# Lent softmax tiles, later weight passes on ScalarE, and low parts on VectorE in an attention and two-layer kernel

## The chip, the cores and the metric

The kernel runs on one core of one Trainium2 chip. The metric is the device time of one execution in microseconds (us). The core has TensorE (matrix products), VectorE and ScalarE (elementwise work and reductions), GpSimd (elementwise work, on-chip memory only) and SyncE, whose queue issues every transfer of this kernel. Each engine runs its own instructions in order, and engines wait for each other by semaphores. In the rows they are PE (PEld is its loading of weights), DVE, ACT, POOL and SP.

## The reference

Attention over `q`, `k`, `v` of shape (4, 8, 576, 64), as the sum of two branches, and then two feed-forward layers over the 2304 tokens, 512 wide with 2048 hidden columns:

```python
# pooled branch: means of 4 neighbours, dense softmax attention over 144 positions, repeated 4 times
out_up = np.repeat(sm_attn(q_d, k_d, v_d), 4, axis=2)
# local branch: softmax over the positions closer than 4
mask = np.abs(pos[:, None] - pos[None, :]) < 4
out_local = softmax(where(mask, scale * q @ k.T, -1e9)) @ v
x = (out_up + out_local)            # (4 * 576 tokens, 512)
h = x @ moe_w_in;  r = np.maximum(h, 0.0);  x = (r * r) @ moe_w_out
h = x @ moe2_w_in; g = h * np.cos(h);       y = g @ moe2_w_out
```

The feed-forward weights arrive as 64-bit floats. The kernel makes of each a 32-bit value and splits it in a high and a low part, and splits the inputs of each product likewise: three products (high by high, high by low, low by high) stand for one.

## The kernel before, in words

**Tokens and blocks.** The local branch works in 36 windows of 64 query tokens, the pooled branch in 16 units (4 batches by 4 head pairs, `down`). The first layer takes the tokens in five blocks of 8, 7, 7, 7 and 7 windows (512 or 448 tokens), and for each block its 16 groups of hidden columns: 80 steps. A step is `stage_a` (line 691: the hidden block, 12 products), `gelem1` on ScalarE (relu in line 715, square in 716, high copy `gh` in 703), `low` on VectorE (line 709, `gl`), and one step or two later `stage_b1` (line 774, 12 products). The second layer follows from about 540 us on.

**Block one comes first.** Before the 80 steps a loop advances all of block one's tasks together, one piece of each in a pass: `pool(0)`, `early_v` (loads of the values and the pooled values' sums, line 283), four `down` units, eight `window` tasks and the conversion of the first three weight blocks. A window is: scores on TensorE (lines 455 and 465), maximum on VectorE (line 339), exponentials on ScalarE (lines 343 or 354), sums and reciprocals on VectorE (356, 477, 478), normalisation on GpSimd (479), transposes (489), a copy (492), the product with the values (510), and on VectorE the sum with the pooled branch (`xt`, line 526); every second window then gives the high part `xh` (537) and the low part `xl` (538) of the layer's input. The product with the values waits until all four `down` units of the batch are done. A window holds a tile `pr` (four there are) from its exponentials to its transposes and a tile `pt` (two) from there to the product of line 510. The sums of line 283 are queued behind the latest traced maximum:

```python
        with behind("max"):
            nc.vector.tensor_reduce(out=vp[...], in_=places[hp]..., op=ALU.add, axis=AX.X)
```

`behind(*names)` puts an instruction behind the last traced one of the first of these names that exists, on the same engine; no semaphore is added by it.

**Weights.** `conv1(f)` loads one raw block of the first layer (1 MB, line 550, two buffers) and `split` converts it: line 564 on ScalarE (a first pass over the upper words), lines 566, 569 and 571 on VectorE (clamp, shift, join with the lower words), line 577 on ScalarE (the high part), line 584 on GpSimd (two subtractions of 128x512, the low parts). The raw buffer is free after line 571. Low parts go to rings of three and five buffers (`LO_RING`) and are also written to memory (line 609), from where the later blocks load them. Blocks 0 to 2 belong to the loop before the steps, blocks 3 to 15 are started at steps 0 to 11. `conv2` does the same with the second layer's weights in steps 18 on, with its low part in line 580 on GpSimd.

**Order.** The program is traced in the order of the Python loops; the framework's planner then orders each engine's queue by a simulated timeline, keeping the order that `behind` asks for. `gelem1` is traced with high priority. The flag `early[0]` is true until the loop for block one has ended. The tiles `gt`, `gl` (two each) and `gh` (three) are the first layer's g tiles, 128x512; the first of them is asked for by step 0.

Of the kernel before, what the change touches and what calls it, by code (L numbers as in the profile page):

```python
# [8 lines left out]
F32 = mybir.dt.float32  # L9
F32R = mybir.dt.float32r  # L10
BF16 = mybir.dt.bfloat16
U32 = mybir.dt.uint32
AF = mybir.ActivationFunctionType
ALU = mybir.AluOpType
# [4 lines left out]
P = 128  # L19
# [4 lines left out]
HPAIR = H // 2  # L24
WQ = 64
WK = WQ + 2 * HALO
# [8 lines left out]
TMAX = 512  # L35
# [31 lines left out]
def window_of(w):  # L67
    b, i = divmod(w, NWB)
    t0 = i * WQ
    k0, k1 = max(t0 - HALO, 0), min(t0 + WQ + HALO, S)  # L70
    return b, i, t0, k0, k1
# [3 lines left out]
def kernel(  # L75
# [11 lines left out]
    nc = tc.nc  # L87
# [4 lines left out]
    gp = ctx.enter_context(tc.tile_pool(name="gp", bufs=3))  # L92
# [9 lines left out]
    cm = cm_pool.__enter__()  # L102
# [10 lines left out]
    for t, v in zip(magic, (MAGIC, -MAGIC)):  # L113
# [9 lines left out]
    caps = {  # L123
        "a": 3, "h": 1, "acc": 4, "qkw": 3, "vw": 3, "pr": 4, "pt": 2, "xt": 2, "qp": 1, "xd": 2, "vp": 1, "av": 3, "pl": 2, "raw": 2,
        "dpr": 2, "dpt": 1, "qk0": 0,
    }
    used = dict.fromkeys(caps, 0)
    now = [-1]
    early = [True]
    kinds = {}  # L130
    last = {}

    def need(name, n=1):
        while early[0] and name in SPREAD:
            if name not in ("qk0", "pl") and used[name] < caps[name]:
                used[name] += 1
                held.setdefault(name, []).append(None)
                return
            if spare:
                held.setdefault(name, []).append(spare.pop(0))  # L140
                return
            other = LENT.get(name)
            if other and used[other] < caps[other]:
                used[other] += 1
                held.setdefault(name, []).append(other)
                return
            yield
        while used[name] + n > caps[name]:
            yield
        used[name] += n  # L150

    def done(name, n=1):
        f = taken[name].pop(0) if early[0] and name in SPREAD else None
        if f is None:
            used[name] -= n
        elif f in caps:
            used[f] -= n
        else:
            spare.append(f)
# [15 lines left out]
    def need_a(n=1):  # L175
        while True:
            free = ["a"] * (caps["a"] - used["a"])
            if early[0]:
                free += [t for tag in ("h", "acc") for t in [tag] * (caps[tag] - used[tag])]
            if len(free) >= n:  # L180
                break
            yield
        got = []
        for tag in free[-n:]:
            used[tag] += 1
            t = {"a": ps_a, "h": ps_h, "acc": ps_acc}[tag].tile([P, 512], F32, tag=tag, name="ps_" + tag)
            kinds[id(t)] = (tag, t)
            got.append(t)
        return got

    def done_a(*ts):
        for t in ts:
            used[kinds.pop(id(t))[0]] -= 1
# [230 lines left out]
    def x_tiles(j):  # L424
        while j > 1 and now[0] < NF * (j - 1) - 1:
            yield
        if j not in xblk:
            xblk[j] = tuple(xp.tile([P, NK, TMAX], F32R, tag=t, name=t) for t in ("xh", "xl"))
        return xblk[j]

    def window(w):
        b, i, t0, k0, k1 = window_of(w)
        n, off = k1 - k0, HALO - (t0 - k0)
# [11 lines left out]
            yield  # L445
        if not early[0]:
            yield
        yield from need("pr")
        while apart and len(whole) < 2 * HPAIR:
            yield  # L450
        s, = yield from need_a()
# [18 lines left out]
                    done("qk0")  # L470
        else:
            done("qkw")
        mx = cm.tile([P, 2, HPAIR], F32, tag="mx", name="mx", bufs=4)
        pr = cm.tile([P, HPAIR, WK], F32, tag="pr", name="pr", bufs=caps["pr"])
        prv = pr[:, :, :n]
        yield from exps(s, sv, mx, prv, SCALE, w % 2 == 0 if apart else w < W0[2])
        nc.vector.tensor_scalar_add(out=mx[:, 1], in0=mx[:, 1], scalar1=1e-9)
# [2 lines left out]
            out=prv, in0=prv, in1=mx[:, 1].unsqueeze(2).broadcast_to([P, HPAIR, n]), op=ALU.mult  # L480
        ).ins
        yield
        if not early[0]:
            yield
        yield from need("pt")
        tp, = yield from need_a()
        tpv = tp.rearrange("p (h m) -> p h m", h=HPAIR)
        for hp in range(HPAIR):
            last["pe"] = nc.tensor.transpose(tpv[:n, hp], pr[:, hp, :n], ident).ins  # L489
        done("pr")  # L490
        pt = cm.tile([WK, HPAIR, P], F32, tag="pt", name="pt", bufs=caps["pt"])
        nc.scalar.copy(out=pt[:n], in_=tpv[:n])
        done_a(tp)
        yield
# [9 lines left out]
        xh, xl = yield from x_tiles(j)  # L504
        av, = yield from need_a()
        avv = av[:, :HPAIR * WQ].rearrange("p (h m) -> p h m", h=HPAIR)
        for hp in range(HPAIR):
            for a in range(2):
# [2 lines left out]
                    avv[rows, hp], vw[:n, hp * P + a * D:hp * P + (a + 1) * D], pt[:n, hp, a * WQ:(a + 1) * WQ],  # L511
                    start=True, stop=True,
                ).ins
        done("pt")
        if not apart:
            done("vw")
        placed[0] += 1
# [2 lines left out]
        if (j, m // 2) not in xts:  # L520
# [6 lines left out]
            out=xt[:, :, (m % 2) * WQ:(m % 2 + 1) * WQ].rearrange("p h (j r) -> p h j r", r=FACTOR),  # L527
            in0=avv.rearrange("p h (j r) -> p h j r", r=FACTOR), in1=xa, op=ALU.add,
# [4 lines left out]
        if m % 2 or m == WINS1[j] - 1:  # L533
            m0 = m - m % 2
            cs = slice(m0 * WQ, (m + 1) * WQ)
            xv = xt[:, :, :(m % 2 + 1) * WQ]
            last["xh"] = nc.scalar.activation(out=xh[:, :, cs], in_=xv, func=AF.Copy).ins
            last["xl"] = nc.vector.tensor_tensor(  # L538
                out=xl[:, :, cs], in0=xv, in1=xh[:, :, cs].bitcast(F32), op=ALU.subtract
# [13 lines left out]
    def behind(*names):  # L553
        for name in names:
            if name in last:
                return tc.issue_after(last[name])
        return nullcontext()

    def split(raw, hi, los=None, sums=None):
        low, top = raw[:, :, 0], raw[:, :, 1]  # L560
        x = rawp.tile([P, 2 * DM], U32, tag="bits", name="bits")
        xv = x.bitcast(F32)
        with behind("relu", "xh", "exp"):
            nc.scalar.activation(out=xv, in_=top.bitcast(F32), func=AF.Prelu, scale=TOP_SCALE, alpha=TOP_ALPHA)
        with behind("gl", "xl"):
            nc.vector.tensor_scalar(  # L566
                out=xv, in0=xv, scalar1=TOP_MAX, scalar2=-TOP_MAX * TOP_ALPHA, op0=ALU.min, op1=ALU.max
            )
        nc.vector.tensor_scalar(out=x, in0=x, scalar1=3, scalar2=None, op0=ALU.logical_shift_left)  # L569
        yield  # L570
        nc.vector.scalar_tensor_tensor(  # L571
            out=x, in0=low, scalar=29, in1=x, op0=ALU.logical_shift_right, op1=ALU.bitwise_or
        )
        if sums:
            yield from sums(xv)
        yield "read"
        nc.scalar.activation(out=hi, in_=xv, func=AF.Copy)
        yield
        if los is None:
            nc.gpsimd.tensor_tensor(out=xv, in0=xv, in1=hi.bitcast(F32), op=ALU.subtract)  # L580
        else:
            for k, lo in enumerate(los()):
                cs = slice(k * DM, (k + 1) * DM)
                nc.gpsimd.tensor_tensor(out=lo, in0=xv[:, cs], in1=hi[:, cs].bitcast(F32), op=ALU.subtract)
        return xv

    hi1 = [None] * NF
# [108 lines left out]
    def g_tile(name, dtype=F32, tag=None):  # L696
        tag = tag or name
        return gp.tile([P, TMAX], dtype, tag=tag, name=name, bufs=3 if tag == "gh" else 2)

    def high(gt):  # L700
        n = gt.shape[1]
        gh = g_tile("gh", F32R)[:, :n]
        nc.scalar.activation(out=gh, in_=gt, func=AF.Copy)  # L703
        return gt, gh

    def low(gt, gh):
# [354 lines left out]
    for i in range(n2 + 4):  # L1061
        j, p = divmod(i, NP2)
# [104 lines left out]
```

## Time and profile before

| | |
|---|---|
| three runs | 942.91, 943.47, 943.68 us, median 943.47 |
| profiled execution | 942.37 us, its span 940.6 us |
| granted TensorE clock, mean | 0.988 |
| busy, share of span | TensorE 97%, VectorE 67%, ScalarE 62%, GpSimd 15% |
| chain that ended last | TensorE 80%, VectorE 10%, transfers 5%, ScalarE 3% |
| moved | 222.78 MB, mean 237 GB/s |

The span is from the first to the last instruction; the execution's time has some 1.8 us around it. A share of the span is an average: the start, where the attention and the conversion of weights run beside TensorE's first products, has other limits than the layers behind it. The chain is followed back from the last instruction to what released each step. A matmul's length as listed overlaps the next one's; the distance of their starts is what one takes.

### The profile page before, as it was taken

How to read it: one execution, taken by the hardware profiler on the slowest of the kernel's cores; microseconds unless marked ns; L12 is line 12 of the kernel's file. 1: busy time of each engine (PE TensorE's matmuls, PEld its weight loads, DVE VectorE, ACT ScalarE, POOL GpSimd, SP SyncE). 2: the span in 40 equal slices, each digit the busy share in tenths (PEclk: the TensorE clock that was granted, in tenths of full speed). 3: DMA queues.
4: the chain of work that ended last, by engine and by line, in shares of the span. 5: the costliest groups of instructions: out<-in, count | busy, mean ns of one | idle time of the engine just before them, and what ended most of it. 6: DMA issues, size and time to landing. Idle time of an engine off the chain costs nothing.

```text
span 940.6 us, 17687 instructions
## 1 busy us (share of the span) xinstructions
PE 913.5 (97%) x6892; PEld 834.8 (89%) x6892; DVE 634.8 (67%) x1181; ACT 579.0 (62%) x1024; POOL 144.7 (15%) x115
## 2 busy tenths in 40 slices
PE   7889979999999999999999999999999999999997
PEld 4667767888989889889899999999999999999997
DVE  7877975764567644454331158879787887888786
ACT  5677756455555555554553377777767777677674
POOL 2336642031131322222220000000000000000000
PEclk9989989999999999999999999999999999999999
DMA  9778885684889857877888886565565565665673
GB/s 232 228 239 310 293 267 175 220 304 155 311 284 316 293 183 266 306 251 260 290 299 295 270 324 208 185 197 201 184 204 190 190 211 189 206 200 186 212 237 102
DMA packets 74224, 222.78 MB, mean 237 GB/s; under 512 B 8932, under 2 KB 14436, under 8 KB 69916
## 3 DMA queue, kind: packets, MB, share of 16 engines
q1 hardware_dynamic: 74140, 221.64, 70.7%
q8 instruction: 54, 0.88, 0.4%
q14 instruction: 30, 0.25, 0.1%
HBM read 180.72 MB, written 40.89 MB: 236 GB/s over the span
## 4 chain that ended last, share of the span: by engine, by line
PE 80%; DVE 10%; DMA 5%; ACT 3%; issue 1%; SPq 0%; POOL 0%; DVEq 0%; ACTq 0%; POOLq 0%
PE ps_h L726 22%; PE acc L798 18%; PE ps_h L691 17%; PE acc L774 16%; DMA pl<-in_pool_v_dram 2%; DVE bits L571 2%; PE ps_a L510 1%; DVE bits L566 1%; DVE gl L709 1%; PE ps_a L489 1%; PE ps_a L465 1%; DMA raw<-in_w_dram 1%; DMA pl<-in_pool_qk_dram 1%; DMA qk<-in_pool_qk_dram 1%; DVE bits L569 1%
## 5 line engine op out<-in xcount | busy, mean ns | idle before, releaser
L726 PE MATMUL ps_h<-x,w2hi 128*128 128x256 f32 x1152 | 159.9, 281 | 0.0
L709 DVE TENSOR_TENSOR gl<-gt,gh 128x448 fp32r<-128x448 f32 (+1 forms) x80 | 61.2, 766 | 129.4 <-ACT gh L703 72.3
L726 PEld LDWEIGHTS ps_h<-x,w2hi 128*128 128x128 f32 x1152 | 146.6, 188 | 0.1
L798 PE MATMUL acc<-bl,gh 128*128 128x256 f32 x504 | 140.5, 280 | 0.0
L691 PE MATMUL ps_h<-xh,w1hi 128*128 128x448 f32 (+1 forms) x320 | 123.8, 388 | 2.5 <-ACT gt L715 2.5
L691 PE MATMUL ps_h<-xl,w1hi 128*128 128x448 f32 (+1 forms) x320 | 122.0, 381 | 1.8 <-DVE xl L538 1.8
L774 PE MATMUL acc<-gl,w1hi 128*128 128x448 f32 (+1 forms) x320 | 120.2, 376 | 0.7 <-DVE gl L709 0.7
L715 ACT ACTIVATE gt<-ps_h 128x448 f32<-128x448 f32 (+1 forms) x80 | 44.2, 553 | 103.3 <-PE ps_h L691 103.0
L774 PE MATMUL acc<-gh,w1hi 128*128 128x448 f32 (+1 forms) x320 | 105.9, 377 | 0.0
L798 PEld LDWEIGHTS acc<-bl,gh 128*128 128x128 f32 x504 | 95.0, 188 | 0.0
L774 PE MATMUL acc<-gh,lo 128*128 128x448 f32 x256 | 93.8, 366 | 0.0
L766 DVE TENSOR_TENSOR gl<-g,gh 128x896 fp32r<-128x896 f32 x72 | 78.2, 1086 | 11.0 <-ACT gh L761 11.0
L798 PE MATMUL acc<-w2hi,gh 128*128 128x256 f32 x288 | 80.9, 281 | 0.0
L734 ACT ACTIVATE u<-ps_h,quarter 128x512 f32<-128x512 f32 x72 | 49.4, 686 | 51.0 <-PE ps_h L726 50.7
L798 PE MATMUL acc<-w2hi,gl 128*128 128x256 f32 x288 | 80.3, 281 | 0.0
L741 DVE SCALAR_TENSOR_TENSOR r<-u,ps_h 128x512 f32<-128x512 f32 x72 | 49.4, 687 | 40.0 <-ACT u L736 34.5
L761 ACT ACTIVATE gh<-g 128x896 fp32r<-128x896 f32 x72 | 68.1, 946 | 10.7 <-DVE g L759 10.6
L746 ACT ACTIVATE r<-r,half_pi 128x512 f32<-128x512 f32 x72 | 51.8, 720 | 33.8 <-DVE r L742 33.8
L691 PEld LDWEIGHTS ps_h<-xh,w1hi 128*128 128x128 f32 x320 | 61.2, 191 | 10.8 <-ACT gt L715 3.2
L691 PEld LDWEIGHTS ps_h<-xl,w1hi 128*128 128x128 f32 x320 | 61.4, 192 | 9.2 <-DVE xl L538 2.3
L726 PE MATMUL ps_h<-x,w2lo 128*128 128x256 f32 x432 | 68.8, 281 | 0.0
L774 PEld LDWEIGHTS acc<-gl,w1hi 128*128 128x128 f32 x320 | 60.3, 188 | 7.8 <-DVE gl L709 1.1
(143 smaller groups left out, 1987.4 us busy)
## 6 DMA issues: line engine op xcount, KB each, us to landing
bl<-wo_d SPq DMA_DIRECT2D x70, 896.0 KB
raw<-in_w_dram SPq DMA_DIRECT2D x32, 1024.0 KB
lo<-lo_d SPq DMA_DIRECT2D x128, 256.0 KB
qkw<-in_win_qk_dram SPq DMA_DIRECT2D x28, 268.0 KB
pl<-in_pool_qk_dram SPq DMA_DIRECT2D x24, 288.0 KB
wo_d<-raw SPq DMA_DIRECT2D x16, 384.0 KB
out_dram<-o SPq DMA_DIRECT2D x18, 256.0 KB
lo_d<-loa SPq DMA_DIRECT2D x16, 256.0 KB
```

The lines of the kernel that those rows point to most:

```text
L571: nc.vector.scalar_tensor_tensor(out=x, in0=low, scalar=29, in1=x, op0=ALU.logical_shift_right, op1=ALU.bitwise_or)
L691: nc.tensor.matmul(h[:, :n], a[:, c * P:(c + 1) * P], x[:, c, :n], start=i == 0, stop=i == len(order) - 1)
L709: last["gl"] = nc.vector.tensor_tensor(out=gl, in0=gt, in1=gh.bitcast(F32), op=ALU.subtract).ins
L715: last["relu"] = nc.scalar.activation(out=gt, in_=h, func=AF.Relu).ins
L726: nc.tensor.matmul(h[:, s * TB:(s + 1) * TB], a[:, c * P:(c + 1) * P], x[:, c], start=i == 0, stop=i == len(order) - 1,)
L734: nc.scalar.activation(out=u, in_=h, func=AF.Identity, bias=quarter, scale=float(1.0 / (2 * math.pi)))
L741: nc.vector.scalar_tensor_tensor(out=r, in0=u, scalar=-PI2_HI, in1=hv, op0=ALU.mult, op1=ALU.add)
L746: nc.scalar.activation(out=r, in_=r, func=AF.Sin, bias=half_pi, scale=1.0)
L761: nc.scalar.activation(out=gh, in_=g[:, 1:], func=AF.Copy)
L766: nc.vector.tensor_tensor(out=gl, in0=g[:, 1:], in1=gh.bitcast(F32), op=ALU.subtract)
L774: nc.tensor.matmul(acc[d][:, :n], a, x, start=f == 0 and i == 0, stop=f == NF - 1 and i == 2)
L798: nc.tensor.matmul(o, a[:, x], b, start=opens and i == 0, stop=p == NP2 - 1 and i == 2 and (k % 2 == 1 or k == NPROD - 1),)
```

## The change

Three edits. (1) While block one is made, a window's `pr` tile may also be one of `gt`, `gt`, `gl`, `gl`, and its `pt` tile one of three `gh`; `band_tile` gives out the tiles in the order in which they come back, and the small tile `mx` of maxima and sums has eight buffers in place of four. (2) In `split`, used for both layers' weights, ScalarE's first pass is queued behind the latest high copy of g (`last["hi"]`) in place of the latest relu, and the high copy of the weights, which had no such order, behind the same. Where no g exists yet, `xh` and `exp` take its place for the first pass, as before, and `xh` for the copy. (3) The two subtractions of line 584 go to VectorE once block one's loop has ended, for weight blocks 3 to 15; blocks 0 to 2 stay on GpSimd, and so does line 580.

```diff
+    lent = {"pr": ["pr"] * caps["pr"] + ['gt', 'gt', 'gl', 'gl'], "pt": ["pt"] * caps["pt"] + ['gh', 'gh', 'gh']}
+
+    def band_tile(name, shape):
+        while early[0] and not lent[name]:
+            yield
+        if not early[0]:
+            yield from need(name)
+        tag = lent[name].pop(0) if early[0] else name
+        if tag == name:
+            return tag, cm.tile(shape, F32, tag=name, name=name, bufs=caps[name])
+        t = gp.tile([P, TMAX], F32R if tag in ("gh", "gl") else F32, tag=tag, name=name, bufs=3 if tag == "gh" else 2)
+        n = shape[1] * shape[2]
+        return tag, t.bitcast(F32)[:shape[0], :n].rearrange("p (a b) -> p a b", a=shape[1])
+
+    def band_done(name, tag):
+        if early[0]:
+            lent[name].append(tag)
+        else:
+            done(name)
...
-        yield from need("pr")
+        pr_tag, pr = yield from band_tile("pr", [P, HPAIR, WK])
...
-        mx = cm.tile([P, 2, HPAIR], F32, tag="mx", name="mx", bufs=4)
-        pr = cm.tile([P, HPAIR, WK], F32, tag="pr", name="pr", bufs=caps["pr"])
+        mx = cm.tile([P, 2, HPAIR], F32, tag="mx", name="mx", bufs=8)
...
-        yield from need("pt")
+        pt_tag, pt = yield from band_tile("pt", [WK, HPAIR, P])
...
-        done("pr")
-        pt = cm.tile([WK, HPAIR, P], F32, tag="pt", name="pt", bufs=caps["pt"])
+        band_done("pr", pr_tag)
...
-        done("pt")
+        band_done("pt", pt_tag)
...
-        with behind("relu", "xh", "exp"):
+        with behind("hi", "xh", "exp"):
             nc.scalar.activation(out=xv, in_=top.bitcast(F32), func=AF.Prelu, scale=TOP_SCALE, alpha=TOP_ALPHA)
...
-        nc.scalar.activation(out=hi, in_=xv, func=AF.Copy)
+        with behind("hi", "xh"):
+            nc.scalar.activation(out=hi, in_=xv, func=AF.Copy)
...
-                nc.gpsimd.tensor_tensor(out=lo, in0=xv[:, cs], in1=hi[:, cs].bitcast(F32), op=ALU.subtract)
+                eng = nc.gpsimd if early[0] else nc.vector
+                eng.tensor_tensor(out=lo, in0=xv[:, cs], in1=hi[:, cs].bitcast(F32), op=ALU.subtract)
...
-        nc.scalar.activation(out=gh, in_=gt, func=AF.Copy)
+        last["hi"] = nc.scalar.activation(out=gh, in_=gt, func=AF.Copy).ins
```

## Rows read from the trace of the kernel before

**Rows 1.** Stretches: PE, PEld, DVE, ACT, POOL busy us (instructions), clock, DMA share, GB/s.

```profile
12.00:50.60 38.60, 29.51 (x430) 22.63 (x428) 34.44 (x79) 26.84 (x90) 15.94 (x17) 0.91 0.83 233
...
62.00:72.00 10.00, 10.00 (x56) 7.36 (x56) 10.00 (x16) 6.46 (x18) 2.55 (x2) 1.00 0.68 212
...
90.00:100.00 10.00, 10.00 (x57) 7.57 (x55) 10.00 (x15) 7.88 (x17) 3.88 (x3) 1.00 0.67 245
...
51.00:143.00 92.00, 83.73 (x511) 65.24 (x511) 71.12 (x109) 63.74 (x155) 44.50 (x33) 0.93 0.80 271
143.00:930.00 787.00, 785.60 (x5878) 737.50 (x5877) 517.94 (x971) 483.37 (x770) 82.46 (x61) 1.00 0.70 235
```

**Rows 2.** Timeline of PE, 14 to 52 us: start, us, instruction [idle before].

```profile
23.86 1.07 PE L489 MATMUL ps_acc<-const_sb,pr 128*70 128x128 f32 x4 [0.31 <-POOL pr L479]
...
33.22 1.07 PE L489 MATMUL ps_acc<-const_sb,pr 128*70 128x128 f32 x8
...
50.62 0.80 PE L691 MATMUL ps_h<-xl,w1hi 128*128 128x512 f32 x1 [1.82 <-DVE xl L538]
```

**Rows 3.** Timeline of DVE, 19 to 31 us.

```profile
19.41 0.41 DVE L339 TENSOR_REDUCE mx<-ps_acc 128x4 f32<-128x280 f32 x1
...
26.35 0.45 DVE L339 TENSOR_REDUCE mx<-ps_acc 128x4 f32<-128x280 f32 x1 [3.46 <-PE ps_acc L465]
...
27.43 3.46 DVE L283 TENSOR_REDUCE vp<-pv 72x256 f32<-72x1024 f32 x3
```

**Rows 4.** Timeline of ACT, 126 to 134 us.

```profile
126.53 0.60 ACT L715 ACTIVATE gt<-ps_h 128x512 f32<-128x512 f32 x1
130.91 1.14 ACT L564 ACTIVATE bits<-raw 128x1024 f32<-128x1024 f32 x1 [3.78 <-DMA raw<-in_w_dram]
131.96 0.61 ACT L716 ACTIVATE gt<-gt 128x512 f32<-128x512 f32 x1
132.47 1.04 ACT L577 ACTIVATE w1hi<-bits 128x1024 fp32r<-128x1024 f32 x1
133.42 0.61 ACT L703 ACTIVATE gh<-gt 128x512 fp32r<-128x512 f32 x1
```

**Rows 5.** Timeline of DVE, 133 to 138 us.

```profile
134.07 1.39 DVE L709 TENSOR_TENSOR gl<-gt,gh 128x512 fp32r<-128x512 f32 x1 [4.50 <-ACT gh L703]
135.38 1.75 DVE L566 TENSOR_SCALAR bits<-bits 128x1024 f32<-128x1024 f32 x1
...
```

**Rows 6.** Timeline of PE, 130 to 147 us.

```profile
137.52 0.44 PE L455 MATMUL ps_a<-const_b 64*64 64x280 bf16 x2 [5.48 <-DVE xt L526]
```

**Rows 7.** Timeline of ACT, 78 to 88 us.

```profile
81.10 1.06 ACT L577 ACTIVATE w1hi<-bits 128x1024 fp32r<-128x1024 f32 x1
```

**Rows 8.** Timeline of PE, 80 to 92 us.

```profile
80.78 0.69 PE L691 MATMUL ps_h<-xh,w1hi 128*128 128x512 f32 x1 [1.82 <-ACT gt L715]
...
86.69 0.39 PE L691 MATMUL ps_h<-xh,w1hi 128*128 128x512 f32 x1
```

**Rows 9.** Groups by form, DVE, 51 to 143 us: busy us, mean ns, idle before.

```profile
L571 DVE SCALAR_TENSOR_TENSOR bits<-raw,bits 128x1024 uint32<-128x1024 uint32 x12 | 17.5, 1467 | 0.2
L566 DVE TENSOR_SCALAR bits<-bits 128x1024 f32<-128x1024 f32 x12 | 13.4, 1123 | 7.5 <-ACT bits L564 7.5
L709 DVE TENSOR_TENSOR gl<-gt,gh 128x512 fp32r<-128x512 f32 x11 | 10.8, 983 | 4.6 <-ACT gh L703 4.5
```

**Rows 10.** Groups by form, DVE, 146 to 300 us.

```profile
L571 DVE SCALAR_TENSOR_TENSOR bits<-raw,bits 128x1024 uint32<-128x1024 uint32 x7 | 8.5, 1220 | 0.1
...
L566 DVE TENSOR_SCALAR bits<-bits 128x1024 f32<-128x1024 f32 x7 | 4.8, 685 | 0.0
...
L709 DVE TENSOR_TENSOR gl<-gt,gh 128x512 fp32r<-128x512 f32 x5 | 3.4, 688 | 2.8 <-ACT gh L703 2.8
```

**Rows 11.** Groups by form, POOL, 51 to 157 us.

```profile
L584 POOL TENSOR_TENSOR loa<-bits,w1hi 128x512 fp32r<-128x512 f32 x14 | 20.0, 1429 | 44.5 <-ACT w1hi L577 19.8 <-issue 13.9 <-PE ps_h L691 5.8
```

**Rows 12.** Waits, POOL, 51 to 157 us: us in total, times, longest.

```profile
POOL loa L584 <- DMA lo_d<-lob: 4.2, 1, 4.2
```

## The prediction

> **What bounds the kernel now.** I read the table of stretches first, because a share over the whole span mixes a start that waits with a long middle that does not. From 143 to 930 us TensorE is busy 785.6 of 787.0 us at full clock [rows 1]: 1.4 us are to be had there, and nothing that the change touches there (ScalarE's passes over the second layer's weights) is late for TensorE. So the change is worth what it does before 143 us. There, from 51 to 143 us, TensorE is busy 83.73 of 92.00 us at a mean clock of 0.93 [rows 1], and before that it can't do the first layer at all, since its input is not there: the first multiplication that needs the last piece of block one's input starts at 50.62 us, after 1.82 us of waiting for VectorE [rows 2].
>
> Next the timelines of the start, for what block one's eight windows wait for. VectorE takes the maximum of window three at 19.41 us and of the next window only at 26.35 us, after 3.46 us without work, and three of the four pooled values' sums follow at 27.43 us, behind that maximum [rows 3]. The reason is in TensorE's timeline: a fifth window gets a probability tile only when one of the four in hand has been transposed, and the second of those transposes starts at 23.86 us; the third and fourth start at 33.22 us [rows 2], when a transposed tile (there are two) has been used by its product with the values. So the windows go through in pairs, and the pooled branch, which every window needs, goes through behind the third pair's maximum.
>
> The third view is the three engines around the largest wait. TensorE stands 5.48 us until 137.52 us for VectorE's sum in line 526 [rows 6]. In ScalarE's order the relu of a g block at 126.53 us is followed by the first weight pass (line 564), which waits 3.78 us for its transfer and starts at 130.91 us; the square, another block's high copy (line 577) and the copy of g follow it, the last at 133.42 us [rows 4]. VectorE waits 4.50 us for that copy, then does line 709 and line 566, and comes to line 526 after that [rows 5]. By count the pass at 130.91 us is the one for weight block 14, whereas TensorE is at block 11: it could have waited.
>
> **Part one: the lent tiles.** Four more probability tiles and three more transposed ones let all eight windows be scored, reduced and normalised before the pooled branch is done, and the pooled sums stand behind a maximum that comes sooner. The work is the same, only its order changes, so the gain is VectorE's missing work. From 12.00 to 50.60 us VectorE is busy 34.44 of 38.60 us [rows 1]: 4.2 us are free. If the order fills them and the three early weight blocks stay ahead of the input's end, the input is complete at 46.4 instead of 50.6 us. If the third block's passes (1.22 us, 0.69 us and one more like the second, as in [rows 10]: 2.6 us) fall behind it, 6.8 us are gained. Against: the maxima of windows four to seven now stand ahead of the pooled sums; at 0.45 us each [rows 3] that is 1.8 us on the pooled branch, the bound on the side of a loss. ScalarE, at 26.84 of 38.60 us [rows 1], has room for the exponentials. I take -4.2 us, since the row for it is the idle itself, and keep -6.8 and +1.8. What is late next is VectorE with no idle at all. The g tiles themselves are asked for by the first layer only after the input is complete, when all eight windows are through: no wait there.
>
> **Part two: ScalarE's passes behind the high copy.** At 126 us the order becomes relu (0.60), square (0.61), copy (0.61) [rows 4], which ends at about 128.4 us, and only then the pass that waits until 130.91 us. VectorE does line 709 before 130.3 us, 0.69 us long [rows 10]; line 566 still stands ahead of line 526, but starts when the pass ends (130.91 + 1.14 = 132.05 us) and takes 0.69 us, and line 526 can end at about 133.2 us. In the trace of before VectorE reached it at 135.38 + 1.75 = 137.13 us, and TensorE went on at 137.52. That is 4.2 us. Bounds: nothing, if another late transfer stands ahead of another relu, and 5.5 us, the whole wait [rows 6]. The price is that every first pass and high copy comes a square and a copy later, 1.2 us. Weight block 5's high copy ends at 82.16 us and its first use is at 86.69 us [rows 7, 8]: 4.5 us of cover hide it at nothing; where the cover is gone it is 1.2 us once, since the passes then follow one another at the same distance.
>
> **Part three: the low parts on VectorE.** Blocks 3 to 15 give 26 subtractions of 128x512. The same operation on the same kinds of operands takes 0.688 us on VectorE where GpSimd does nearly none of them [rows 10], so 17.9 us are added to VectorE, nearly all from 51 to 143 us. What comes back: in that stretch line 571 takes 1.467 us (1.220 later), line 566 1.123 us (0.685 later) and line 709 0.983 us (0.688 later) [rows 9, 10]. Times 12, 12 and 11 that is 3.0 + 5.3 + 3.2 = 11.5 us, and I take all of it as time in which GpSimd's subtractions held VectorE up. The net is +6.4 us on VectorE, which has 92.00 - 71.12 = 20.9 us free in the stretch; it is without a gap in 62 to 72 and in 90 to 100 us [rows 1], 20 of 92 us. I charge that share: 6.4 x 0.22 = +1.4 us. From below: -1.8 us, if the earlier low parts end the wait of 1.82 us at 80.78 us [rows 8]. From above: GpSimd stood 5.8 us for TensorE and 4.2 us for a write to memory before it could overwrite a ring buffer [rows 11, 12]; it lost nothing by that, but VectorE, waiting in the same place, would hold back line 709's low parts of g and the sums for the windows behind it, and TensorE waits for both: +10.0 us. SyncE's writes of the low parts, and the weight transfers queued behind these, come when the subtraction ends, 1.4 us after the high copy instead of 2.9 (twice 1.43, [rows 11]); I count nothing for that, since the next transfer also waits for line 571.
>
> The GPSIMD Engine Reference of the Trainium skill (section Key points) says that GpSimd shares its interfaces to the on-chip memory with VectorE, and that they contend where VectorE has two such inputs or runs in a mode with two ports. The trace agrees: line 709, with two inputs, takes 0.983 us beside GpSimd and 0.688 us without. Were the long durations due to something else that stays, VectorE would get 17.9 us instead of 6.4, the charge would be 3.9 us and the sum -4.5.
>
> **The sum.** -4.2 - 4.2 + 1.4 = -7.0 us. The profiled execution took 942.37 us with a span of 940.6; the median of the three runs is 943.47, 1.1 us more. So 942.37 - 7.0 + 1.1 = 936.5 us.
>
> **The rivals.**
> - *All of it comes.* The third block's passes fall behind the input and both waits go: -6.8 - 5.5 - 1.8 = -14.1 us, 929.4 us. For it: TensorE is short of work in no other place. Against: each place has to come out well in an order that the planner draws up anew.
> - *The weights hold.* The input is early, but the raw weights come through two buffers and one queue of transfers, and TensorE, with 4.5 us of cover at block 5, only waits for them sooner; the late transfer of 130 us stops it elsewhere. Both gains are given back and the 1.4 us stay: 944.9 us. For it: the wait at 130 us began with a transfer. Against: the weights from block 3 on are started by the first g block, so they move up with the input.
> - *VectorE waits for the ring (the other side).* A subtraction on VectorE stands before a buffer that TensorE or a write still holds, and what is behind it in the queue is what TensorE needs: +10.0 us. It falls where blocks 11 to 14 are made, so that part two's gain is not had: -4.2 + 10.0 = +5.8 us, 949.3 us. It decides once such a wait is longer than TensorE's cover, 4.5 us at block 5. For it: GpSimd's two waits of 5.8 and 4.2 us. Against: the planner knows these waits and can put other work ahead.
> - *The lending does nothing.* Windows are scored early, but the pooled branch or ScalarE sets the input's end: 0 - 4.2 + 1.4 = -2.8 us, 940.7 us.
>
> **How the numbers follow.** Forecast 0.48 (its own range 932 to 940.5 us), all of it 0.12, weights 0.17, ring 0.14, no lending 0.09. A difference under 0.2%, 1.9 us, can't be told from none: faster is below 941.6 us, slower above 945.4. Faster: 0.46 + 0.12 + 0.02 from the weights case + 0.06 from the last = 0.66. Same: 0.01 + 0.13 + 0.01 + 0.03 = 0.18. Slower: 0.01 + 0.02 + 0.13 = 0.16. The range 929 to 946 leaves out half of the first rival and most of the third, 0.06 + 0.12.
>
> **What would show it.** Part one: window seven's maximum before 24 us, no wait of VectorE near 23 us, and the first multiplication with the low part of the input near 46 us. Part two: no line 564 between a relu and its copy, and no wait of some 5 us of TensorE for line 526. Part three: line 571 near 1.22 us throughout from 55 us on, and VectorE's idle time in front of line 584 under 2 us in all; waits there of 4 us and more, with TensorE waiting for line 709 or 526 behind them, would make the forecast wrong, and so would a first multiplication no earlier than 49 us.

## The result, and the profile after

The changed kernel takes 933.72 us (median of 4 runs, 931.59 to 938.64) beside 943.58 for the kernel before on the same chip (4 runs, 942.91 to 948.2). The ratio is 0.987 [0.983, 0.991], and the difference of the medians is 9.9 us. The forecast was 936.5 with an own range of 932 to 940.5, so it came out 2.8 us faster than forecast, inside that range. Once more on another chip, run `e5_after_again` below, the ratio was 0.988 [0.985, 0.992].

The profiled execution of after is its slowest, 938.64 us with a span of 936.6. The table of stretches shows where it differs: TensorE's granted clock from 12 to 50.6 us was 0.82, beside 0.96 in `e5_after_again`, and its second hidden block starts 2.1 us later (56.30 against 54.20 us). So the profile of `e5_after_again`, the same kernel with 934.0 us and a span of 931.9, stands beside it. Numbers of the lines have moved: 691 is 711, 774 is 794, 709 is 729, 703 is 723, 715 is 735, 716 is 736, 564 is 582, 566 is 584, 571 is 589, 577 is 596, 584 is 604, 526 is 544, 537 and 538 are 555 and 556, 339 is 359, 283 is 303, 390 and 406 are 410 and 426, 455 is 475, 465 is 485, 479 is 498, 489 is 508, 492 is 510, 510 is 528.

Stretches of after (columns as in [rows 1]), the counterpart of [rows 1], with two more, from 62 to 143 and from 143 to 200 us:

```profile
12.00:50.60 38.60, 32.86 (x436) 27.73 (x435) 30.78 (x78) 26.93 (x91) 13.35 (x15) 0.82 0.79 216
...
51.00:143.00 92.00, 87.42 (x539) 68.33 (x538) 78.43 (x135) 68.78 (x154) 13.58 (x12) 0.96 0.82 285
...
62.00:143.00 81.00, 81.00 (x522) 63.65 (x522) 70.22 (x121) 62.46 (x133) 7.21 (x6) 1.00 0.82 286
...
143.00:200.00 57.00, 54.12 (x405) 45.53 (x404) 35.40 (x77) 28.41 (x70) 9.51 (x10) 1.00 0.78 263
```

The stretch of `e5_after_again` from 12 us to the end of its last `xl`, as [rows 1] ends with that of before:

```profile
12.00:46.74 34.74, 26.93 (x430) 22.41 (x427) 29.59 (x76) 25.36 (x90) 12.92 (x14) 0.95 0.82 223
```

From 62 to 143 us TensorE has no gap left (81.00 of 81.00 us at full clock). There the view of waits for before has two, the 5.48 us of [rows 6] and the 1.8 us of [rows 8]; for after it has none. These two waits cost before more than their length. Stretches of before, the whole from 62 to 143 us and one behind each wait:

```profile
62.00:143.00 81.00, 73.58 (x442) 57.35 (x442) 66.28 (x96) 54.35 (x127) 41.30 (x29) 0.94 0.81 273
81.00:84.00 3.00, 3.00 (x8) 2.32 (x8) 3.00 (x6) 2.36 (x5) 2.45 (x3) 0.50 0.85 330
138.00:141.00 3.00, 3.00 (x21) 2.48 (x18) 3.00 (x9) 1.50 (x5) 0.00 (x0) 0.50 0.90 279
```

Behind each wait the granted clock was 0.50, the lower of its two levels (1.2 and 2.4 GHz), and products of 128x512 started 0.43 us apart, where they start 0.23 us apart from 87 us and from 143 us on. By the timeline this lasts from 80.78 to about 84.3 us and from 137.5 to about 142.0; half of that, some 4 us, is an estimate of what it cost.

GpSimd's 44.50 us of work from 51 to 143 us has become 13.58, and VectorE's 71.12 has become 78.43: +7.3 by all three edits together. From 143 to 200 us TensorE is busy 54.12 of 57.00 us, where before has it busy throughout: 2.9 us are given back there, in waits of at most 1.1 us for a product's issue, GpSimd and g's copy.

Timeline of PE, `e5_after_again`, 19 to 57 us, against [rows 2]:

```profile
22.54 0.65 PE L485 MATMUL ps_acc<-qk,qk 64*64 64x70 f32 x16
...
24.10 0.92 PE L410 MATMUL ps_acc<-const_sb,dpr 96*72 96x96 f32 x6 [0.37 <-POOL pr L498]
26.30 0.41 PE L410 MATMUL ps_acc<-const_sb,dpr 96*72 96x96 f32 x3 [1.28 <-POOL pr L498]
...
29.50 3.45 PE L508 MATMUL ps_acc<-const_sb,pr 128*67 128x128 f32 x20
...
46.07 0.50 PE L711 MATMUL ps_h<-xh,w1hi 128*128 128x512 f32 x1 [1.44 <-ACT xh L555]
46.80 0.50 PE L711 MATMUL ps_h<-xl,w1hi 128*128 128x512 f32 x1 [0.23 <-DVE xl L556]
...
54.20 0.80 PE L711 MATMUL ps_h<-xh,w1hi 128*128 128x512 f32 x1 [4.57 <-ACT gt L735]
```

The windows no longer go in pairs: the last scores start at 22.54 us, the transposes of five windows run as one group of 20 from 29.50 us on, and those of the other three follow from 38.61 us. The first product with `xl` starts at 46.80 us (50.62 in [rows 2]). New is a wait of 4.57 us for the first relu, in front of the second hidden block; from 54 to 57 us, behind it, the granted clock is 0.50 here too.

Timeline of DVE, `e5_after_again`, 19 to 52 us, against [rows 3]:

```profile
25.24 0.44 DVE L359 TENSOR_REDUCE mx<-ps_acc 128x4 f32<-128x280 f32 x1
25.60 4.58 DVE L303 TENSOR_REDUCE vp<-pv 72x256 f32<-72x1024 f32 x4
...
36.93 1.29 DVE L544 TENSOR_TENSOR xt<-ps_acc,xd 128x256 f32<-128x256 f32 x3 [2.82 <-PE ps_acc L528]
...
46.05 0.69 DVE L556 TENSOR_TENSOR xl<-xt,xh 128x512 fp32r<-128x512 f32 x1 [0.69 <-ACT xh L555]
...
48.67 1.25 DVE L584 TENSOR_SCALAR bits<-bits 128x1024 f32<-128x1024 f32 x1
...
51.77 1.23 DVE L589 SCALAR_TENSOR_TENSOR bits<-raw,bits 128x1024 uint32<-128x1024 uint32 x1
```

The last maximum is at 25.24 us with the pooled sums right behind it. The 3.46 us without work of [rows 3] are gone, and 2.82 us for TensorE have come at 36.93 us. The passes of the third weight block, at 45.17 to 48.88 us before, stand behind the last `xl` here, from 48.67 us on.

Timeline of ACT, after, 118 to 134 us, against [rows 4]:

```profile
118.12 1.12 ACT L582 ACTIVATE bits<-raw 128x1024 f32<-128x1024 f32 x1 [1.84 <-DMA raw<-in_w_dram]
119.15 1.04 ACT L596 ACTIVATE w1hi<-bits 128x1024 fp32r<-128x1024 f32 x1
120.10 0.58 ACT L735 ACTIVATE gt<-ps_h 128x512 f32<-128x512 f32 x1
120.58 0.38 ACT L417 COPY dpt<-ps_a 72x288 f32<-72x288 f32 x1
120.85 0.64 ACT L736 ACTIVATE gt<-gt 128x512 f32<-128x512 f32 x1
121.52 0.63 ACT L723 ACTIVATE gh<-gt 128x512 fp32r<-128x512 f32 x1
```

Relu, square and copy follow one another with a small copy between them; the pass that waits for a transfer (1.84 us at 118.12) stands ahead of a relu, not behind it.

Groups by form, DVE, after, 51 to 143 us, against [rows 9]:

```profile
L589 DVE SCALAR_TENSOR_TENSOR bits<-raw,bits 128x1024 uint32<-128x1024 uint32 x14 | 17.7, 1261 | 0.1
L584 DVE TENSOR_SCALAR bits<-bits 128x1024 f32<-128x1024 f32 x14 | 10.2, 725 | 6.3 <-ACT bits L582 6.3
...
L729 DVE TENSOR_TENSOR gl<-gt,gh 128x512 fp32r<-128x512 f32 x13 | 8.9, 682 | 3.0 <-ACT gh L723 3.0
L604 DVE TENSOR_TENSOR loa<-bits,w1hi 128x512 fp32r<-128x512 f32 x12 | 8.2, 684 | 0.6 <-ACT w1hi L596 0.5
L604 DVE TENSOR_TENSOR lob<-bits,w1hi 128x512 fp32r<-128x512 f32 x12 | 8.2, 682 | 0.0
```

The three lines of [rows 9] went from 1467, 1123 and 983 ns to 1261, 725 and 682, and the new subtractions take 0.68 us each, with 0.6 us of idle time in front of them in all. Of the waits for a ring buffer in [rows 11, 12] VectorE took over none.

### The profile page after: what moved, and what is told of

Same layout as the page of the kernel before. It is cut to its first block, busy times and chain, and to the rows that moved or that the text cites. A ratio compares the mean times of both kernels' runs of the same rounds, so it can differ in the third digit from the quotient of the medians.

```text
span 936.6 us, 17648 instructions
## 1 busy us (share of the span) xinstructions
PE 913.4 (98%) x6886; PEld 835.4 (89%) x6886; DVE 638.6 (68%) x1207; ACT 580.4 (62%) x1024; POOL 108.6 (12%) x89
## 4 chain that ended last, share of the span: by engine, by line
PE 87%; DVE 5%; DMA 5%; ACT 2%; issue 1%; POOL 0%; DVEq 0%; POOLq 0%; ACTq 0%
PE ps_h L746 22%; PE ps_h L711 19%; PE acc L794 19%; PE acc L818 18%; DMA pl<-in_pool_v_dram 3%; DMA pl<-in_pool_qk_dram 2%; PE ps_a L528 1%; PE ps_warm L931 1%; PE ps_a L485 1%; PE ps_a L508 1%; PE ps_a L389 1%; PE ps_a L426 1%; PE ps_a L410 1%; PE acc L816 1%; PE ps_acc L528 1%; DVE mx L359 1%
## 5 line engine op out<-in xcount | busy, mean ns | idle before, releaser
L729 DVE TENSOR_TENSOR gl<-gt,gh 128x448 fp32r<-128x448 f32 (+1 forms) x80 | 56.2, 703 | 131.2 <-ACT gh L723 67.4
L794 PE MATMUL acc<-gh,w1hi 128*128 128x448 f32 (+1 forms) x320 | 111.2, 377 | 2.2 <-ACT gh L723 2.2
L794 PEld LDWEIGHTS acc<-gh,w1hi 128*128 128x128 f32 x320 | 59.6, 188 | 9.4 <-ACT gh L723 2.7
```

The costliest lines, as they stand in the source:

```text
L729: last["gl"] = nc.vector.tensor_tensor(out=gl, in0=gt, in1=gh.bitcast(F32), op=ALU.subtract).ins
L794: nc.tensor.matmul(acc[d][:, :n], a, x, start=f == 0 and i == 0, stop=f == NF - 1 and i == 2)
```

## The experiments

Every run was timed beside the kernel before, on three chips (`e1` to `e4`, `e5` to `e8`, `e9` to `e12`), on which before took 948.9, 946.7 and 947.1 us in the median (24, 14 and 29 executions). The ratios are those on record; they are not quotients of these medians. Parts: L = the lent tiles, O = ScalarE's order, V = low parts on VectorE.

Executions of one kernel differ in TensorE's mean granted clock, and the kernels without lent tiles have many at a low one, before 42 of 67 (last section). So the last column gives the median of those executions alone that have a mean of 0.988 or more, and how many they are; by the same choice before has 944.1 us (25 of 67). This is called like clock below.

| run | what it is | us | ratio | us at like clock |
|---|---|---|---|---|
| e1_lend_only | before + L | 942.32 | 0.9956 [0.9924, 0.9987] | 942.3 (7 of 7) |
| e2_no_lend | before + O + V | 941.70 | 0.9917 [0.9888, 0.9946] | 938.4 (3 of 9) |
| e3_order_only | before + O | 940.61 | 0.9925 [0.9894, 0.9955] | 939.6 (6 of 9) |
| e4_low_only | before + V | 946.05 | 0.9984 [0.9961, 1.0008] | 944.6 (9 of 12) |
| e5_after_again | before + L + O + V | 933.72 | 0.9883 [0.9845, 0.9921] | 933.7 (6 of 6) |
| e6_no_order | before + L + V | 938.45 | 0.9925 [0.9893, 0.9957] | 938.5 (9 of 9) |
| e7_no_low | before + L + O | 935.24 | 0.9895 [0.9862, 0.9929] | 935.2 (6 of 6) |
| e8_late_exp | after, exponentials later | 934.91 | 0.9893 [0.9859, 0.9928] | 934.9 (6 of 6) |
| e9_before_warm6 | before, more junk products | 942.54 | 0.9947 [0.9926, 0.9969] | 942.5 (12 of 12) |
| e10_after_warm6 | after, more junk products | 937.96 | 0.9900 [0.9871, 0.9928] | 938.0 (6 of 6) |
| e11_pass_only | before + half of O | 945.21 | 0.9980 [0.9955, 1.0004] | 944.4 (9 of 12) |
| e12_copy_only | before + other half of O | 944.76 | 0.9979 [0.9953, 1.0005] | 944.5 (10 of 12) |

### The three parts, each by itself and each left out

`e1`, `e3` and `e4` put one part of the change into before, `e2`, `e7` and `e6` leave one out of after. Their edits are the parts of the diff above: L is `lent`, `band_tile`, `band_done` and the eight `mx`; O is

```diff
-        with behind("relu", "xh", "exp"):
+        with behind("hi", "xh", "exp"):
...
-        nc.scalar.activation(out=hi, in_=xv, func=AF.Copy)
+        with behind("hi", "xh"):
+            nc.scalar.activation(out=hi, in_=xv, func=AF.Copy)
...
-        nc.scalar.activation(out=gh, in_=gt, func=AF.Copy)
+        last["hi"] = nc.scalar.activation(out=gh, in_=gt, func=AF.Copy).ins
```

and V is the two lines with `eng`.

> Of the three edits only the lent tiles. As predicted: the input of block one complete 4.2 us sooner, 939.3 us beside 943.5 before. Theory from the trace of after (the pooled branch ended at 36.6 us instead of 33.3, the input only 1.7 us sooner, and 4.6 us of waiting followed): within 1.5 us of before, 942 to 945 us.

> The other two edits without the lent tiles. As predicted: -4.2 + 1.4 = -2.8 us, 940.7 us. Theory from the trace of after (the gain lies between 62 and 143 us, where TensorE lost 16.2 us before and 5.5 us after): some 10 us less than before, 932 to 935 us. If the edits only act together through a new order of the queues, neither.

> Of the three edits only ScalarE's order (weight passes behind g's high copy). As predicted: the wait of 5.48 us at 137.52 shrinks by 4.2 us, 939.3 us. Rival, the low parts on VectorE are what ends the waits: the wait stays or moves, 942 to 945 us.

> Of the three edits only the low parts of weight blocks 3 to 15 on VectorE. As predicted: +1.4 us, 944.9 us, with line 571 near 1.22 us from 55 us on. Rival, the low parts are what ends the waits: 4 us or more less than before, 939.5 us or less. Ring waits on VectorE: 949 us, with 4 us and more of idle time ahead of line 584.

> The changed kernel once more, beside the others on one chip. If the three edits add up as measured alone (0.9956 x 0.9925 x 0.9984), 0.987 of before. In the profile, if the spread between executions comes from TensorE's clock in the first 60 us, a run with a higher mean clock is a faster one, by some 0.6 us for each 0.001.

> The changed kernel without ScalarE's order: lent tiles and low parts on VectorE. If the edits add up (0.9956 x 0.9984), 0.994 of before. As predicted: -4.2 + 1.4 = -2.8 us, 0.997. If the gain comes from any new order of the queues, near 0.987.

> The changed kernel with all low parts of layer one on GpSimd: lent tiles and ScalarE's order. If the edits add up (0.9956 x 0.9925), 0.988 of before. As predicted: -8.4 us, 0.991. If the low parts on VectorE are what makes the other two pay, 0.993 or more.

With `e5` and before these are all eight combinations. Each part can be added in four of them, and the ratio falls by

- L: 0.0044 (to nothing), 0.0030 (to O), 0.0059 (to V), 0.0034 (to O + V): mean 0.0042, 3.9 us of 943.6
- O: 0.0075 (to nothing), 0.0061 (to L), 0.0067 (to V), 0.0042 (to L + V): mean 0.0061, 5.8 us
- V: 0.0016 (to nothing), 0.0031 (to L), 0.0008 (to O), 0.0012 (to L + O): mean 0.0017, 1.6 us

At like clock the same four differences are 1.8, 4.3, 6.2 and 4.6 us for L (mean 4.2), 4.6, 7.1, 6.3 and 4.7 us for O (5.7), and -0.5, 3.9, 1.2 and 1.5 us for V (1.5).

The three alone multiplied give 0.9956 x 0.9925 x 0.9984 = 0.987; after has 0.987 in the first comparison and 0.988 in `e5`. So, as far as these intervals tell, the parts add up and none needs another. The intervals reach about 0.003 to either side, so V by itself is not told from nothing. By ratio all four of its differences have one sign, which speaks for a small gain; at like clock before with V alone is 0.5 us slower than before.

### Which half of the order works

> The kernel before with only the first weight pass (line 564) behind g's high copy; the weights' high copy as before. As predicted for the order, whose gain was the pass that waits for its transfer between a relu and its copy: all of it, 0.992 to 0.995 of before. Rival, it is the high copy of the weights standing ahead of g's copy: 0.998 or more.

> The kernel before with only the weights' high copy (line 577) behind g's high copy; the first pass behind the relu as before. As predicted: little, 0.998 or more of before. Rival: 0.992 to 0.995.

`e11` puts only the first pass (564) behind g's high copy, `e12` only the weights' high copy (577), each with the line that sets `last["hi"]`:

```diff
-        with behind("relu", "xh", "exp"):
+        with behind("hi", "xh", "exp"):
```

```diff
-        nc.scalar.activation(out=hi, in_=xv, func=AF.Copy)
+        with behind("hi", "xh"):
+            nc.scalar.activation(out=hi, in_=xv, func=AF.Copy)
```

By ratio each brought 0.002, with an interval that reaches 1, and both together (`e3`) 0.0075. At like clock neither brought anything: 944.4 and 944.5 us beside 944.1 of before, where `e3` has 939.6. The timeline of ACT, `e11`, 118 to 134 us, shows why the pass alone does not do:

```profile
120.73 0.62 ACT L715 ACTIVATE gt<-ps_h 128x512 f32<-128x512 f32 x1
124.02 1.06 ACT L577 ACTIVATE w1hi<-bits 128x1024 fp32r<-128x1024 f32 x1 [2.68 <-DVE bits L571]
124.99 0.61 ACT L716 ACTIVATE gt<-gt 128x512 f32<-128x512 f32 x1
125.63 0.63 ACT L703 ACTIVATE gh<-gt 128x512 fp32r<-128x512 f32 x1
```

and the same of `e12`, where the pass is free to move:

```profile
129.45 0.58 ACT L716 ACTIVATE gt<-ps_h 128x512 f32<-128x512 f32 x1
131.60 1.14 ACT L564 ACTIVATE bits<-raw 128x1024 f32<-128x1024 f32 x1 [1.57 <-DMA raw<-in_w_dram]
132.65 0.61 ACT L717 ACTIVATE gt<-gt 128x512 f32<-128x512 f32 x1
...
133.64 0.63 ACT L704 ACTIVATE gh<-gt 128x512 fp32r<-128x512 f32 x1
```

Whichever weight instruction is free is put between a relu and its square and waits there: the copy 2.68 us for VectorE's line 571, the pass 1.57 us for its transfer. From relu to the end of `gh` that makes 5.5 us (126.26 - 120.73) and 4.8 us, beside 7.5 in [rows 4] and 2.1 in the fence of after. Between 50 and 176 us the timelines count 7 passes and 4 copies in such a place before, 3 and 7 in `e11`, 6 and 3 in `e12`, 3 and 4 in `e3` with both halves, 2 and 2 after. From 62 to 200 us TensorE's waits add up to 7.3 us before, 7.0 in `e11`, 7.4 in `e12` and 4.6 in `e3`. TensorE keeps its wait for the sum that feeds the next window, in `e11` behind 143 us (waits of PE, 143 to 200 us):

```profile
PE ps_a L455 <- DVE xt L526: 3.4, 1, 3.4
```

and in `e12` (waits of PE, 62 to 143 us):

```profile
PE ps_a L455 <- DVE xt L526: 3.2, 1, 3.2
PE acc L775 <- DVE gl L710: 1.5, 2, 1.2
```

### Taking away the new wait at 54 us

> The changed kernel with block two's windows started two steps later and their exponentials, where they are done one head at a time, queued behind the latest high copy of g. Theory: in the changed kernel the relu of step 0 stood behind eight exponentials of windows eight and nine and TensorE waited 4.58 us for it at 56.3 us, then ran a group at half clock; with the relu ahead of them 3 to 6 us less than the changed kernel, 0.981 to 0.984 of before. Rival: the raw weights hold, TensorE only waits one or two groups later, 0.986 to 0.988.

```diff
-                last["exp"] = nc.scalar.activation(
+                with nullcontext() if early[0] else behind("hi"):
+                    last["exp"] = nc.scalar.activation(
...
-        start_at(m if j == 1 else NF * (j - 1) - 7 + 2 * m, window, w)
+        start_at(m + 2 if j == 1 else NF * (j - 1) - 7 + 2 * m, window, w)
```

In `e5` ScalarE has eight exponentials of block two's windows (from 51.16 us on, the first after 2.63 us of waiting for VectorE) ahead of the first relu:

```profile
53.51 0.63 ACT L735 ACTIVATE gt<-ps_h 128x512 f32<-128x512 f32 x1
```

`e8` starts block two's windows two steps later and puts the exponentials behind g's high copy. The relu moved up to 49.90 us, TensorE's wait of 4.57 us went, and its second hidden block started at 50.55 instead of 54.20 us: 3.7 us earlier. The time did not move: 934.91 beside 933.72 for `e5` on the same chip. The sixth hidden block is still 6.3 us ahead (76.95 against 83.25 us), the twelfth only 1.2 (125.0 against 126.2); in part the hidden blocks are ahead because the windows' work was put off. Stretches of `e8`:

```profile
80.00:110.00 30.00, 27.70 (x172) 21.56 (x171) 26.42 (x51) 23.10 (x58) 6.27 (x5) 0.95 0.84 285
```

and of `e5_after_again`:

```profile
80.00:110.00 30.00, 30.00 (x157) 23.28 (x156) 28.63 (x51) 22.41 (x48) 4.83 (x4) 1.00 0.88 305
```

TensorE lost 2.3 us from 80 to 110 us, and from 55 to 150 us ScalarE's passes waited 6.2 us for raw weights in `e8`, 3.9 in `e5`. So the 3.7 us are given back before the twelfth block. The first passes of weight blocks 3 to 8 start 1.4 to 3.8 us sooner than in `e5`, those of blocks 9 to 15 mostly later (95.77 against 95.06 us for block 9, 133.75 against 132.36 for block 15). This speaks for the rival in which the weights hold, but only for what could be gained beyond this change; that the raw weights alone do it was not tried.

### Is part of the gain TensorE's clock?

> The kernel before with six instead of two junk products on TensorE after each pass of block one's loop that used TensorE. Theory: part of the lent tiles' gain is the granted clock of the first 60 us, which falls to half in a part of the executions without them (mean clock of an execution 0.980 to 0.985, 947 to 954 us) and hardly ever with them; then the slow executions go and the median falls to 942 or 943 us, 0.995 to 0.996 of before. Rival: the clock only follows the waits and the junk products stand in the way: 0.999 or more.

> The changed kernel with six instead of two junk products in the same place. Clock theory: its executions are at 0.992 to 0.994 already, 0 to 2 us to be had, 0.985 to 0.988 of before. Rival: the products delay block one's pooled branch, 2 us or more lost, 0.990.

```diff
-WARM = 2
+WARM = 6
```

`WARM` is the number of junk products that TensorE does between the pieces of block one. Six in place of two make before 5 us faster (0.9947) without any lent tile, but 1.6 us at like clock (942.5 beside 944.1): most of the 5 us is that none of the 12 executions has a mean clock under 0.988. With the lent tiles alone (`e1`) none of 7 has, and there the gain is 4.2 us by ratio and 1.8 us at like clock. The same six make after 4 us slower than `e5` by the medians of the two chips (937.96, 933.72; the ratios, 0.990 and 0.988, differ by less than their intervals). In `e10` the first product of the first layer starts at 48.01 us against 46.07, behind three groups of six junk products of 1.46 to 1.47 us each where two take 0.59.

## Why the prediction was right, and where it was off

**Part one, -4.2 us: the size was right, the reason was not.** In the sum of the parts the lent tiles are worth 3.9 us (4.2 at like clock), and the input is complete at 46.74 us in `e5` where the prediction had 46.4 (50.6 before). But the step "the gain is VectorE's missing work ... if the order fills them" failed. Up to the end of the last `xl` VectorE is idle 4.16 us of 38.60 before [rows 1] and 5.15 of 34.74 in `e5` (34.74 - 29.59): no idle time was filled, 1.0 us was added. What went is work in front of the input, 34.44 - 29.59 = 4.85 us. The third weight block's three passes fell behind it (0.68 + 0.69 + 2.05 us before), which is the mechanism that the prediction kept for its bound of -6.8, and the last `xl` takes 0.69 instead of 1.76 us. 4.85 - 0.99 = 3.86 us, of which 1.9 are left at the second hidden block (54.2 against 56.1 us), behind the new wait of 4.57 us. That this comes so near to 4.2 is luck.

What was left out is TensorE's own queue. The first of the pooled branch's transposes, at 19.35 us before, now stand behind the scores of all eight windows and start at 24.10 us, so the pooled branch's last copy starts at 36.40 instead of 33.06 us, and VectorE waits 2.82 us for the products behind it. The prediction counted the four maxima that move ahead on VectorE (1.8 us) as the only price. The sign "window seven's maximum before 24 us" was missed by 1.2 us for the same reason.

How much of part one comes through TensorE's clock is not settled. At like clock `e1` is 1.8 us under before, and the other three pairs that differ by L alone are 4.3 to 6.2 us apart, each of these over two chips (before at like clock has 944.2 us on the one and 943.8 on the other).

**Part two, -4.2 us: 5.8 measured (5.7 at like clock), mechanism wider than forecast.** That a weight pass which waits for a transfer between relu and copy of g costs TensorE its next window was right; in after no such wait is left from 62 to 143 us. The step named line 564 alone. `e11` and `e12` show that line 577, which waits for VectorE, takes the same place as soon as 564 is barred from it, and that barring either of them leaves a wait of over 3 us. The whole wait of 5.48 us goes, more than the 4.2 us worked out from one place. And the sum put nothing for the clock behind a wait, though the prediction quotes the 0.93 of that stretch: the half clock from 137.5 to about 142.0 us, some 2 us by the estimate above, goes with the wait. How the 5.8 us divide between the two was not tried. The sign "no line 564 between a relu and its copy" was met only in part, since two passes stand there in after. The cover of 4.5 us for a later high copy held: TensorE waits for no weights in after.

**Part three, +1.4 us: the sign was wrong, inside its bounds (-1.8 to +10.0).** The step that failed is the net load of +6.4 us. After has 7.3 us more on VectorE than before from 51 to 143 us, but by all three edits; that the two numbers are near each other is luck. The pairs that differ by V alone give +3.0 us (`e4` less before), +0.9 (`e2` less `e3`), +6.2 (`e6` less `e1`) and -1.7 (`e5` less `e7`) in that stretch. Stretches of `e4`, of `e7` and of `e5`:

```profile
51.00:143.00 92.00, 85.89 (x542) 67.21 (x540) 74.08 (x126) 61.80 (x141) 15.33 (x12) 0.94 0.82 276
```

```profile
51.00:143.00 92.00, 88.40 (x546) 68.40 (x545) 81.43 (x109) 69.05 (x150) 49.06 (x37) 0.98 0.79 277
51.00:143.00 92.00, 88.81 (x548) 69.90 (x549) 79.75 (x141) 71.46 (x163) 11.49 (x11) 0.96 0.82 283
```

`e5` does 26 more subtractions than `e7` here in less time. The prediction let three lines come back; in `e7` the third pass (line 587) also takes 928 ns, beside 686 in `e5`, and a 128x4 operation of line 361 takes 1035 ns in the mean, beside 310. What falls into the stretch differs from run to run; over the whole execution the same pairs give -1.3, +2.8, +4.1 and -1.8 us by their pages, with 26 instructions more. So the net load was smaller than worked out, and the charge of 0.22 of it as time was not tested. The -1.8 us of the lower bound, the wait of [rows 8], are gone, but they are also gone in `e7`, without V (its only wait of PE from 62 to 143 us is 0.5 us for GpSimd). So what the 1.6 us are, if they are more than chance, stays open.

The rival in which VectorE waits for the ring (0.14) is refuted: 0.6 us of idle time in front of line 604, and the 4.9 us in `e4` are for ScalarE's high copy. The one that lending does nothing (0.09) is spoken against by `e1` and the three other pairs, of which `e1` is the weakest (1.8 us at like clock). All of it comes (0.12) asked for 929.4 us; the median came 2.8 of the 7.1 us towards it. For the weights that hold (0.17) see `e8`.

**The sum.** Forecast -4.2 - 4.2 + 1.4 = -7.0. By parts the runs give -3.9 - 5.8 - 1.6 = -11.3, so part three's sign, if its 1.6 us are no chance, makes 3.0 of the 4.3 us between them, part two's size 1.6, and part one 0.3 the other way. By the medians of the first comparison it is -9.9; the 1.4 us between the two measurements lie within the interval of either.

## What to carry to other kernels

An instruction that may wait (for a transfer, or for another engine) does not belong between two links of a chain that TensorE waits for, and all instructions that could slip into that place have to be barred at once: either half of this edit alone brought nothing at like clock, both together 4.6 us. Where a change frees buffers so that work goes through together, look at the queue of every engine that the work shares, TensorE's too: here what was interleaved before now stands behind the whole group. What a load moved from one engine to another adds has to be measured over everything that the first engine held up, not over the costliest lines alone. And a wait of TensorE is priced with the clock that is granted behind it.

## What the runs showed of the hardware

**Executions of one program differ by the clock of their start.** Of before's 67 executions on the three chips, 25 have a mean granted clock of 0.988 or more and a median of 944.1 us; 42 have 0.980 to 0.987 and 949.9 us. From 200 to 930 us the clock is 1.00 in every profile here, so the difference arises before. No profile of before itself was taken at a low mean. From 25 to 40 us this is the line of `e2_no_lend` (mean 0.984), then of `e3_order_only` (0.994) and `e9_before_warm6` (0.990), none of which has lent tiles:

```profile
25.00:40.00 15.00, 13.92 (x147) 10.99 (x148) 9.10 (x18) 7.30 (x21) 1.35 (x3) 0.61 0.80 260
```

```profile
25.00:40.00 15.00, 13.38 (x218) 9.94 (x217) 13.34 (x28) 10.20 (x33) 5.19 (x6) 1.00 0.87 288
```

```profile
25.00:40.00 15.00, 13.65 (x205) 9.77 (x206) 12.00 (x22) 8.55 (x29) 4.96 (x6) 1.00 0.87 283
```

At 0.61 most of the stretch runs at the lower level, TensorE gets through 147 products instead of 218 and is busy all the same, and VectorE and ScalarE get through less. `e4_low_only`, profiled at a mean of 0.985, has 0.69 and 154 products there. In the kernels without lending the lower mean was found in 42 of 67 executions of before, 6 of 9 of `e2`, 3 of 9 of `e3`, 3 of 12 each of `e4` and `e11` and 2 of 12 of `e12`; with lending in none of 40, with six junk products and no lending in none of 12. After's profiled execution shows that the low start has not gone altogether: 0.989 over the whole, 0.82 from 12 to 50.6 us, and 4 to 7 us more than its three other runs. What decides how an execution starts is not shown. So a gain at such a start has to be compared at like clock: `e9` got 5 us with products that compute nothing.

**GpSimd's subtractions held VectorE up.** With them gone and nothing else changed (groups by form, DVE, `e4`, 51 to 143 us, against [rows 9]):

```profile
L571 DVE SCALAR_TENSOR_TENSOR bits<-raw,bits 128x1024 uint32<-128x1024 uint32 x13 | 16.5, 1275 | 0.1
...
L566 DVE TENSOR_SCALAR bits<-bits 128x1024 f32<-128x1024 f32 x13 | 8.8, 684 | 3.5 <-ACT bits L564 3.5
...
L710 DVE TENSOR_TENSOR gl<-gt,gh 128x512 fp32r<-128x512 f32 x11 | 8.0, 724 | 0.6 <-ACT gh L704 0.5
```

Line 566 went from 1.123 to 0.684 us, line 709 (710 here) from 0.983 to 0.724, line 571 from 1.467 to 1.275. The GPSIMD Engine Reference of the Trainium skill (section Key points) says that the two engines share their interfaces to the on-chip memory and contend where VectorE has two such inputs or runs in a mode with two ports. Line 709, with two inputs, agrees; line 566 has one, and in which mode it runs no row here shows.
